# Order and size of the first transfers, and the place of early work, in a sliding-window attention kernel with a feed-forward stage

## The chip, the cores and the metric

The kernel runs on one core of a Trainium2 chip. The core has TensorE (PE: matmuls and transposes into PSUM; its weight loads are listed as PEld), VectorE (DVE), ScalarE (ACT), GpSimd (POOL) and SyncE (SP), each with its own instruction stream, and 16 DMA engines that move data between HBM and SBUF. Streams wait for each other by semaphores. The metric is the device time of one execution in microseconds.

## The reference

Attention over 8 batches of 8 heads, 576 positions, head size 64, where a position sees the positions at most 32 away, followed by a feed-forward layer on the 4608 tokens (512 features, 2048 hidden):

```
scores = q @ k^T / sqrt(64);  masked to |i - j| <= 32
attn   = softmax(scores);     y = attn @ v
x = y with the heads side by side          # 4608 x 512
h = x @ w_in                               # 4608 x 2048
g = h where h >= 1;  0 where h <= -1;  (h + 1)^2 / 4 between
out = g @ w_out                            # 4608 x 512
```

Inputs are float32; the kernel's transfers turn them into bfloat16 on the way in.

## The kernel before, in words

Everything is recorded in a fixed order (a manual schedule): each engine runs its instructions in the order in which the Python code gives them.

**Visits.** The main loop `for a in range(NF * NB + NF)` runs 152 visits. NB = 18 blocks of TB = 256 tokens, NF = 8 groups of 256 hidden columns. Visit a belongs to block t and group f (a = 8t + f). It makes `hp`, 256 hidden values of 256 tokens: 8 matmuls of 128x256 from `xT` (the attention's result, transposed) and 256 columns of `w_in` (line 441). ACT makes `rr` from hp (445), DVE makes `mx` (447) and then `gT` (448), the activated hidden values. So visits 0 and 1 read w_in's columns 0 to 511, visits 2 and 3 those from 512, visits 4 and 5 those from 1024, visits 6 and 7 those from 1536, and visit 8 starts the second block.

**Quarters.** `quarter(x)` (line 412) makes a quarter of the sum over hidden values of 128 output rows: 4 matmuls of 128x512 from gT and one of four pieces of `w_out`; x = 4 * (row group) + piece. After the fourth piece ACT copies the rows (417) and SP stores them. From visit 16 on each visit does the quarter a - 8; for the first two blocks the table `quarters` tells which visit does which. Quarters 3 and 7 are the first that read the fourth piece of w_out.

**Attention.** The long transfers of q and k (`load_long`, line 85) bring the first three batches in halves, four transfers each for q and for k and each half. `tpose` (179, 181) transposes them on TensorE into PSUM in two parts, 5 and 4 groups of columns, with one copy each into `qT` or `kT` (182). `scores` (218) and `scores8` (243) multiply q and k and take the exponential on ACT (226, 249, 251); the mask is either added beforehand by matmuls with `bias` (198, where `eng` is None) or multiplied afterwards by DVE (193, where `eng` is V). `sums` (284) multiplies with v and with ones; its `end` has ACT make the reciprocal in two steps (290, 291) and leaves to `muls` a DVE product that writes `xT` (296, 299); `flush` records the pending products. The table `ev`, filled by `at`, says in which visit each of these steps stands, and `tps` in which visit the transposes stand. Block 0 needs the first 256 positions of batch 0, which are done ahead of the loop; visit 8 needs the rest of batch 0 up to position 512, so the second halves of q and k of batch 0 are transposed in visit 1 and scored in visits 2 and 3, with sums in visits 3 to 5. Visit 16 needs the first sums of batch 1, which stand in visit 15. Two PSUM pools of two banks each, `ps_s` and `ps_n`, serve scores, sums and transposes in turn; `ps_o` holds quarters, and the tiles of visits 6 and 7; `ps_h` the other hp.

**Transfers.** All but the first q go through POOL's queue, in the order of lines 101 to 152: the first half of k and v of batch 0, then the list `w` (w_in in pieces, each half of the partitions apart, line 105) with the second half of q and k of batch 0 mixed in, then w_out (109) and the halves of batches 1 and 2. Later batches are loaded from within the loop (93, 101) and transposed by DMA (186).

**Warming.** `keep_warm` (318) issues matmuls whose results nobody reads.

Of the kernel before, what the change touches and what calls it, by code (L numbers as in the profile page):

```python
# [15 lines left out]
def kernel(  # L16
# [20 lines left out]
    B, H, S, D = q.shape  # L37
# [9 lines left out]

    const = ctx.enter_context(tc.tile_pool(name="const", bufs=1))
    nat = ctx.enter_context(tc.tile_pool(name="nat", bufs=2))
    qjp = ctx.enter_context(tc.tile_pool(name="qjp", bufs=2))  # L50
    ktp = ctx.enter_context(tc.tile_pool(name="ktp", bufs=3))
    ptp = ctx.enter_context(tc.tile_pool(name="ptp", bufs=2))
    smp = ctx.enter_context(tc.tile_pool(name="smp", bufs=2))
# [87 lines left out]
    def halves(b, half):  # L141
        return [(load_long, b, half, t, y) for t in range(2) for y in range(NY)]

    def put(todo):
        for fn, *x in todo:
            fn(*x)

    w = [(load_w_in, c, c + d, h) for c, d in ((0, 256), (256, 256), (512, 512), (1024, 512), (1536, 512)) for h in range(2)]
    x = halves(0, 1)
    put(w[:4] + x[:4] + w[4:5] + x[4:] + w[5:])  # L150
    mix(halves(1, 0), [(load_w_out, 0)])
    put([(load_w_out, 1), (load_w_out, 2)] + [(load_v, 1, n) for n in range(4)])
    mix(halves(1, 1), [(load_w_out, 3)])
# [102 lines left out]
    def sums(b, y1, lo, hi, pool=ps_n):  # L256

        bb = two_banks(pool)
        w = hi - lo
        todo = []  # L260
        if lo < MAIN:
            ys, D0 = (y1,), w
            for par in range(2):
                a0 = max(lo, 32 * par)
                off = 32 - 64 * par
                todo.append((None, a0 - lo, hi - lo, lambda a, h, par=par, a0=a0, off=off: (
                    pt[b][HD[a], h, y1, par, a0 + off:hi + off])))
                for c2 in range(4):
                    q0, q1 = max(0, 128 * c2 - off, lo), min(128 * c2 + 128 - off, hi)
                    if q0 < q1:  # L270
                        todo.append((NC * y1 + 2 * c2 + par, q0 - lo, q1 - lo, lambda a, h, par=par, q0=q0, q1=q1, off=off: (
                            pt[b][HD[a], h, y1, par, q0 + off:q1 + off])))
        else:
            ys, D0 = (0, 1), 2 * w
            todo.append((None, 0, 2 * w, lambda a, h: pt8[b][HD[a], h].rearrange("p y j -> p (y j)")))
            for y in ys:
                todo.append((NC * y + 8, y * w, y * w + w, lambda a, h, y=y: pt8[b][HD[a], h, y]))
                for c in (None, NC * y + 7):
                    todo.append((c, y * w, y * w + 64, lambda a, h, y=y: pt[b][HD[a], h, y, 1, 448:512]))
        for n, (c, c0, c1, p) in enumerate(todo):  # L280
            o = D0 if c is None else 0
            for a in range(2):
                for h in range(2):
                    nc.tensor.matmul(bb[HD[h], a, o + c0:o + c1], ones[HD[a]] if c is None else vn[b][HD[a], c, h],  # L284
                                     p(a, h), start=n == 0, stop=True, skip_group_check=True)

        def end():
            lr = smp.tile([128, 2, 256], FP, name="lr", bufs=1)
            rc = smp.tile([128, 2, 256], FP, name="rc")
            A.activation(lr[:, :, :D0], bb[:, :, D0:2 * D0], AF.Ln)  # L290
            A.activation(rc[:, :, :D0], lr[:, :, :D0], AF.Exp, scale=-1.0)  # L291
            r0 = (b * S + lo) % RING
            o = xT.rearrange("p (a y) t -> p a y t", a=2)[:, :, ys[0]:ys[-1] + 1, r0:r0 + w]
            if len(ys) == 1:
                o = o[:, :, 0]
                muls.append(lambda: V.tensor_mul(o, bb[:, :, :D0], rc[:, :, :D0]))  # L296
            else:
                like = "p a (y j) -> p a y j"
                muls.append(lambda: V.tensor_mul(o, bb[:, :, :D0].rearrange(like, y=2), rc[:, :, :D0].rearrange(like, y=2)))
        return end  # L300

    def flush():
        while muls:
            muls.pop(0)()
# [4 lines left out]
    def tp1(pool):  # L309
        if pool is ps_h:  # L310
            return pool.tile([128, 8, 128], BF, name="tp", tag="hp")
        return pool.tile([128, 2, 8, 128], BF, name="tp", tag="bb")[:, 0]

    def keep_warm(n, pool, tag):

        z = pool.tile([128, 512], FP, name="z", tag=tag)
        for _ in range(n):
            nc.tensor.matmul(z, warm[:, :128], warm, start=True, stop=True)
# [42 lines left out]

    NB = NT // TB
    NF = DFF // 256
    quarters = {11: ([], [0]), 12: ([], [1]), 13: ([], [2]), 14: ([], [4, 5]), 15: ([6], [3, 7])}
    ev, tps = {}, {}

    def at(a, *todo):

        ev.setdefault(a, []).extend(x for x in todo if x)

    def steps(b, cut):

# [2 lines left out]
                yield (sums, b, y1, lo, hi), (scores, b, (y1, y1 + 1), (0, 2), (2 * k, 2 * k + 2))  # L375
        yield (sums, b, 0, MAIN, S), (scores8, b)

    at(2, (scores, 0, (0, 1), (0, 2), (2, 4)), (scores8, 0, ps_o))
    at(3, (sums, 0, 0, TB, MAIN), (scores, 0, (1, 2), (0, 2), (2, 4)))
    at(4, (sums, 0, 1, TB, MAIN, ps_s))  # L380
    at(5, (sums, 0, 0, MAIN, S))
    seq = [x for b in range(1, B) for x in steps(b, 224)]
    at(15, seq[0][0], (*seq[1][0], ps_s))
    for n, a in enumerate((20, 22, 23, 27)):
        at(a, seq[2 + n][0])
    for n, a in enumerate((11, 12, 19, 20, 22, 26, 27)):
        at(a, seq[n][1])
    sl = [30, 32, 35, 39, 42, 45, 49, 52, 56, 59, 62, 65, 69, 73, 77, 81, 84, 88, 92]
    sl += [96, 99, 103, 106, 110, 113, 116, 120, 124, 128]
    for n, a in enumerate(sl):  # L390
        at(a, seq[6 + n][0], seq[7 + n][1] if n < len(sl) - 1 else None)
    for b, half, *a in ((0, 1, 1, 1.5), (1, 0, 9, 10), (1, 1, 17, 18), (2, 0, 24, 25), (2, 1, 28, 29)):
        for t in range(2):
            tps[a[t]] = [(b, 2 * half + part, t) for part in range(2)]
    loads, xps = {}, {}
    for b in range(LONG, B):
        a = sl[5 * (b - 1) - 7] - 17
# [7 lines left out]
    def quarter(x):  # L405

        tt, ff = divmod(x, 4)
        if tt not in op:
            op[tt] = ps_o.tile([128, DM], FP, name="op", tag="op"), []
        o, done = op[tt]  # L410
        for j in range(4 * ff, 4 * ff + 4):
            nc.tensor.matmul(o, gT[tt // 2][:, j, 128 * (tt % 2):128 * (tt % 2) + 128], w_out[:, j],  # L412
                             start=not done, stop=len(done) == 2 * NF - 1, skip_group_check=True)
            done.append(j)
        if len(done) == 2 * NF:
            osb = osp.tile([128, DM], FP, name="osb")
            A.copy(osb, o)  # L417
            nc.sync.dma_start(out=out[128 * tt:128 * tt + 128, :], in_=osb)

    for a in range(NF * NB + NF):  # L420
        t, f = divmod(a, NF)
        eng = None if a < 12 else V
        pre, post = quarters.get(a, ([], [a - NF] if a >= 2 * NF else []))
        for b, x in loads.get(a, []):
            if x < 2:
                load_nat(b, x)
            else:
                for n in range(4):
                    load_v(b, n)
        flush()  # L430
        if t < NB:
            if f == 0:
                gT[t] = gtp.tile([128, 2 * NF, TB], BF, name="gT", tag="gT")
            r0 = TB * t % RING
            if a in (6, 7):
                hp = ps_o.tile([128, 2, TB], FP, name="hp", tag="op")
            else:
                hp = ps_h.tile([128, 2, TB], FP, name="hp", tag="hp")
            for j in range(2):
                for n, kk in enumerate((0, 2, 1, 3)):  # L440
                    nc.tensor.matmul(hp[:, j], w_in[:, kk, 256 * f + 128 * j:256 * f + 128 * j + 128],  # L441
                                     xT[:, kk, r0:r0 + TB], start=n == 0, stop=n == 3)

            rr = ewp.tile([128, 2, TB], FP, name="rr")
            A.activation(rr, hp, AF.Relu, scale=0.5, bias=0.5)  # L445
            mx = ewp.tile([128, 2, TB], FP, name="mx")
            V.tensor_max(mx, hp, rr)  # L447
            V.scalar_tensor_tensor(gT[t][:, 2 * f:2 * f + 2], rr, 1.0, mx, op0=ALU.min, op1=ALU.mult)  # L448
        for x in pre:
            quarter(x)  # L450
        ends = []
        for fn, *x in ev.get(a, []):
            if fn is sums:
                ends.append(sums(*x))
            else:
                pool = (x.pop(),) if x[-1] in (ps_s, ps_n, ps_o) else ()
                fn(*x, eng, *pool)
        for end in ends:
            end()
        for x in post:  # L460
            quarter(x)
        for part in (a, a + 0.5):
            copies = [tpose(b, n, t, (A.copy, V.tensor_copy)[i if a > 15 else 0], tp1((ps_s, ps_n)[i]))
                      for i, (b, n, t) in enumerate(tps.get(part, []))]
            for x in copies:
                x()
        for x in xps.get(a, []):
            xpose(*x)

# [29 lines left out]
```

## Time and profile before

| what | us |
|---|---|
| median of 7 runs (322.29 to 324.14) | 323.01 |
| the profiled execution | 323.01 |
| its span, first to last instruction | 321.2 |
| PE busy in the span | 300.5 |
| DVE busy | 246.6 |
| ACT busy | 194.7 |
| L441 (visits' matmuls), busy | 150.2 |
| L412 (quarters), busy | 137.8 |
| mean granted TensorE clock | 0.992 |

Times in the profile count from the first instruction of the span. A row of the timeline reads: start, length, engine, line, operation, output <- input, shape, count, and in brackets how long the engine had stood idle and what ended it. "Time to landing" of a transfer counts from the start of its issue on the queue's engine to its last byte's signal. The clock is the share of full speed that TensorE was granted.

### The profile page before, as it was taken

The numbers are of one execution on the slowest core, as the hardware profiler recorded it, in microseconds if no ns is written. First come the engines' busy times: TensorE is split into PE (matmuls) and PEld (weight loads), VectorE is DVE, ScalarE is ACT, GpSimd is POOL, SyncE is SP. The second block draws the span as 40 slices with busy tenths as digits, with TensorE's granted clock in tenths as the row PEclk, the third lists the DMA queues.
The fourth block names the chain that finished last, engine by engine and source line by source line (L and its number), as shares of the span: only waits on it lengthen the run. The fifth ranks groups of instructions, "written<-read, shape, count | busy, mean of one in ns | idle before, by whom it ended". The sixth has DMA issues, their size and how long they took to land.

```text
span 321.2 us, 8493 instructions
## 1 busy us (share of the span) xinstructions
PE 300.5 (94%) x3599; PEld 202.4 (63%) x3643; DVE 246.6 (77%) x384; ACT 194.7 (61%) x320; POOL 86.2 (27%) x120
## 2 busy tenths in 40 slices
PE   8949899989999999999999999999999999999995
PEld 3536655566666666666666666666666666666652
DVE  2335975887888898888888888888888888887760
ACT  3648765676776566766666667566666766554421
POOL 8882826998303703221410300000000000000000
PEclk9998999999999999999999999999999999999999
DMA  9999898999999999929991945005320001000111
GB/s 147 139 157 181 126 170 130 193 165 164 151 157 156 169 156 175 165 51 103 190 158 48 109 90 125 35 33 108 81 63 33 35 35 36 33 35 33 47 53 65
DMA packets 121029, 34.52 MB, mean 107 GB/s; under 512 B 108704, under 2 KB 116128, under 8 KB 120992
## 3 DMA queue, kind: packets, MB, share of 16 engines
q0 software_dynamic: 92128, 18.06, 73.0%
q1 hardware_dynamic: 28864, 15.93, 21.5%
q8 instruction: 28, 0.46, 0.6%
q14 instruction: 9, 0.07, 0.1%
HBM read 36.70 MB, written 9.44 MB: 144 GB/s over the span
## 4 chain that ended last, share of the span: by engine, by line
PE 83%; DVE 4%; DMA 3%; ACT 3%; issue 3%; POOL 3%; POOLq 0%; ACTq 0%
PE hp L441 37%; PE op L412 36%; PE bb L284 6%; DMA w_in<-in_moe_w_in_dram 3%; PE bb L218 2%; DVE mx L447 1%; DVE gT L448 1%; PE tp L179 1%; POOL vn L101 1%; POOL kn L85 1%; ACT pt L226 1%; ACT lr L290 1%; ACT rc L291 1%; POOL w_in L105 1%; ACT rr L445 1%
## 5 line engine op out<-in xcount | busy, mean ns | idle before, releaser
L441 PE MATMUL hp<-xT,w_in 128*128 128x256 bf16 x1152 | 150.2, 274 | 2.9 <-DVE xT L296 0.9
L412 PE MATMUL op<-w_out,gT 128*128 128x512 bf16 x534 | 137.8, 379 | 5.8 <-issue 5.4
L445 ACT ACTIVATE rr<-hp 128x512 f32<-128x512 f32 x144 | 85.6, 595 | 91.0 <-PE hp L441 87.6
L441 PEld LDWEIGHTS <-w_in 128*128 128x128 bf16 x1152 | 112.1, 98 | 44.8 <-issue 3.5
L447 DVE TENSOR_TENSOR mx<-hp,rr 128x512 f32<-128x512 f32 x144 | 99.3, 690 | 42.2 <-ACT rr L445 40.0
L448 DVE SCALAR_TENSOR_TENSOR gT<-rr,mx 128x512 bf16<-128x512 f32 x144 | 99.6, 692 | 4.9
L412 PEld LDWEIGHTS <-gT 128*128 128x128 bf16 x576 | 53.3, 98 | 41.7
L226 ACT ACTIVATE pt<-bb 128x1024 bf16<-128x1024 f32 (+1 forms) x33 | 33.1, 1010 | 6.1 <-PE bb L218 4.9
L101 POOL DMA_DIRECT2D vn<-in_v_dram x32 | 27.6, 881 | 27.6 <-PE bb L218 26.5
L296 DVE TENSOR_TENSOR xT<-bb,rc 128x512 bf16<-128x512 f32 (+1 forms) x32 | 21.1, 658 | 11.3 <-ACT rc L291 10.8
L417 ACT COPY osb<-op 128x512 f32<-128x512 f32 x36 | 20.8, 581 | 11.6 <-PE op L412 11.2
L291 ACT ACTIVATE rc<-lr 128x512 f32<-128x512 f32 (+2 forms) x40 | 23.5, 587 | 1.3
L93 POOL DMA_DIRECT2D qn<-in_q_dram x10 | 12.3, 1244 | 41.7 <-DMA qT<-qn 41.7
L290 ACT ACTIVATE lr<-bb 128x512 f32<-128x512 f32 (+2 forms) x40 | 22.0, 550 | 1.5 <-PE bb L284 1.3
L193 DVE TENSOR_TENSOR pt<-pt,mask 128x1024 bf16<-128x1024 bf16 (+1 forms) x34 | 20.9, 616 | 0.2 <-ACT pt L226 0.2
L284 PE MATMUL bb<-pt,ones 64*64 64x256 bf16 (+3 forms) x352 | 19.5, 255 | 1.4 <-DVE xT L296 0.6
L284 PE MATMUL bb<-pt,vn 64*64 64x128 bf16 (+3 forms) x712 | 18.4, 204 | 0.6 <-issue 0.6
L284 PEld LDWEIGHTS <-vn 64*64 64x64 bf16 x712 | 16.8, 107 | 0.8 <-issue 0.8
L284 PEld LDWEIGHTS <-ones 64*64 64x64 bf16 x352 | 10.4, 105 | 10.3 <-issue 9.4
L85 POOL DMA_DIRECT2D kn<-in_k_dram x24 | 13.0, 551 | 12.7 <-DMA w_in<-in_moe_w_in_dram 5.3
L218 PE MATMUL bb<-qT,kT 64*64 64x128 bf16 x520 | 13.4, 220 | 0.8 <-DVE kT L182 0.8
L93 POOL DMA_DIRECT2D kn<-in_k_dram x10 | 12.1, 1223 | 3.3 <-DMA kT<-kn 2.5
(44 smaller groups left out, 97.4 us busy)
## 6 DMA issues: line engine op xcount, KB each, us to landing
out_dram<-osb SPq DMA_DIRECT2D x36, 256.0 KB, 2.3
vn<-in_v_dram POOLq DMA_DIRECT2D x32, 144.0 KB, 6.2
qn<-in_q_dram POOLq DMA_DIRECT2D x10, 288.0 KB, 7.2
kn<-in_k_dram POOLq DMA_DIRECT2D x10, 288.0 KB, 8.5
w_out<-in_moe_w_out_dram POOLq DMA_DIRECT2D x4, 512.0 KB, 10.3
kn<-in_k_dram POOLq DMA_DIRECT2D x24, 72.0 KB, 4.4
w_in<-in_moe_w_in_dram POOLq DMA_DIRECT2D x6, 256.0 KB, 7.2
qn<-in_q_dram POOLq DMA_DIRECT2D x20, 72.0 KB, 4.7
```

The costliest lines, as they stand in the source:

```text
L93: nc.gpsimd.dma_start(out=x[:, :, h], in_=src[b, NY * h:NY * h + NY].rearrange("y s d -> (y s) d") .rearrange("(u p) d -> p u d", p=128))
L101: nc.gpsimd.dma_start(out=vn[b][64 * a:64 * a + 64, :, h], in_=v[b, y:y + 2].rearrange("y s d -> (y s) d") .rearrange("(c r) d -> r c d", ...
L226: A.activation(p, ps[:, :, :128 * n].rearrange(like, y=m), AF.Exp, scale=D ** -0.5)
L284: nc.tensor.matmul(bb[HD[h], a, o + c0:o + c1], ones[HD[a]] if c is None else vn[b][HD[a], c, h], p(a, h), start=n == 0, stop=True, skip_g ...
L290: A.activation(lr[:, :, :D0], bb[:, :, D0:2 * D0], AF.Ln)
L291: A.activation(rc[:, :, :D0], lr[:, :, :D0], AF.Exp, scale=-1.0)
L296: muls.append(lambda: V.tensor_mul(o, bb[:, :, :D0], rc[:, :, :D0]))
L412: nc.tensor.matmul(o, gT[tt // 2][:, j, 128 * (tt % 2):128 * (tt % 2) + 128], w_out[:, j], start=not done, stop=len(done) == 2 * NF - 1, s ...
L441: nc.tensor.matmul(hp[:, j], w_in[:, kk, 256 * f + 128 * j:256 * f + 128 * j + 128], xT[:, kk, r0:r0 + TB], start=n == 0, stop=n == 3)
L445: A.activation(rr, hp, AF.Relu, scale=0.5, bias=0.5)
L447: V.tensor_max(mx, hp, rr)
L448: V.scalar_tensor_tensor(gT[t][:, 2 * f:2 * f + 2], rr, 1.0, mx, op0=ALU.min, op1=ALU.mult)
```

## The change

1. **Transfers.** The piece of w_in with columns 512 to 1023 is cut in two pieces of 256 columns (w_in's transfers go from 10 to 12). The second halves of q and k of batch 0 are issued together behind the four transfers of columns 0 to 511; before, q stood there, then one transfer of 512 columns, then k.
2. **Visit 1.** The second parts of q and k are copied out of PSUM by DVE instead of ACT, and four warming matmuls stand between q's transposes and k's.
3. **Visits 3 to 5.** The second scores of visit 3 go ahead of the sums there and use the pool ps_n; the three sums use ps_s, ps_n, ps_s. In visits 1 to 5 the pending products are recorded behind the visit's gT, and not at its start.
4. **Visits 9 to 15.** Quarters 0 and 4 move to visits 9 and 11 and quarters 1, 5, 2, 6 to 12, 13, 13, 14; 3 and 7 stay in 15. The scores of visits 11 and 12 go behind the visit's quarter, and both add their mask by matmuls (the border for `eng` moves from 12 to 14).
5. The transposes of later halves are entered in `ev` at half positions (9.5 and so on), which `run` serves behind the quarters as `tps` did. The unused pool `qjp` goes. From visit 16 on the order of instructions on PE, ACT and DVE is the same.

```diff
-    w = [(load_w_in, c, c + d, h) for c, d in ((0, 256), (256, 256), (512, 512), (1024, 512), (1536, 512)) for h in range(2)]
-    x = halves(0, 1)
-    put(w[:4] + x[:4] + w[4:5] + x[4:] + w[5:])
+    w = [(load_w_in, c, c + d, h) for c, d in ((0, 256), (256, 256), (512, 256), (768, 256), (1024, 512), (1536, 512))
+         for h in range(2)]
+    put(w[:4] + halves(0, 1) + w[4:])
...
-    quarters = {11: ([], [0]), 12: ([], [1]), 13: ([], [2]), 14: ([], [4, 5]), 15: ([6], [3, 7])}
+    quarters = [(9, 0), (11, 4), (12, 1), (13, 5), (13, 2), (14, 6), (15, 3), (15, 7)]
...
+    def through(b, half, t):
+        return [(tpose, b, 2 * half + part, t, part) for part in range(2)]
...
+    at(1, *through(0, 1, 0), (keep_warm, 4, ps_o, "op"))
+    at(1.5, *through(0, 1, 1))
     at(2, (scores, 0, (0, 1), (0, 2), (2, 4)), (scores8, 0, ps_o))
-    at(3, (sums, 0, 0, TB, MAIN), (scores, 0, (1, 2), (0, 2), (2, 4)))
-    at(4, (sums, 0, 1, TB, MAIN, ps_s))
-    at(5, (sums, 0, 0, MAIN, S))
+    at(3, (scores, 0, (1, 2), (0, 2), (2, 4), ps_n), (sums, 0, 0, TB, MAIN, ps_s))
+    at(4, (sums, 0, 1, TB, MAIN))
+    at(5, (sums, 0, 0, MAIN, S, ps_s))
...
-    for n, a in enumerate((11, 12, 19, 20, 22, 26, 27)):
+    for n, a in enumerate((11.5, 12.5, 19, 20, 22, 26, 27)):
         at(a, seq[n][1])
...
+    def run(pos):
+        todo = []
+        for fn, *x in ev.get(pos, []):
+            if fn is sums:
+                todo.append(sums(*x))
+            elif fn is tpose:
+                part = x.pop()
+                todo.append(tpose(*x, (A.copy, V.tensor_copy)[part if pos < 2 or pos > 16 else 0], tp1((ps_s, ps_n)[part])))
+                if part:
+                    while todo:
+                        todo.pop(0)()
+            elif fn is keep_warm:
+                keep_warm(*x)
+            else:
+                pool = (x.pop(),) if x[-1] in (ps_s, ps_n, ps_o) else ()
+                fn(*x, eng, *pool)
+        for end in todo:
+            end()
...
-        eng = None if a < 12 else V
+        eng = None if a < 14 else V
...
-        flush()
+        if a == 0 or a > 5:
+            flush()
...
+        flush()
+        run(a)
         for x in post:
             quarter(x)
-        for part in (a, a + 0.5):
-            copies = [tpose(b, n, t, (A.copy, V.tensor_copy)[i if a > 15 else 0], tp1((ps_s, ps_n)[i]))
-                      for i, (b, n, t) in enumerate(tps.get(part, []))]
-            for x in copies:
-                x()
+        run(a + 0.5)
```

More of the change, by code (lines that the diff above doesn't have):

```diff
@@ L49 @@
     nat = ctx.enter_context(tc.tile_pool(name="nat", bufs=2))
-    qjp = ctx.enter_context(tc.tile_pool(name="qjp", bufs=2))
     ktp = ctx.enter_context(tc.tile_pool(name="ktp", bufs=3))
@@ L363 @@
     NF = DFF // 256
-    quarters = {11: ([], [0]), 12: ([], [1]), 13: ([], [2]), 14: ([], [4, 5]), 15: ([6], [3, 7])}
-    ev, tps = {}, {}
+    quarters = [(9, 0), (11, 4), (12, 1), (13, 5), (13, 2), (14, 6), (15, 3), (15, 7)]
+    ev = {}
     def at(a, *todo):
         ev.setdefault(a, []).extend(x for x in todo if x)
+    def through(b, half, t):
+        return [(tpose, b, 2 * half + part, t, part) for part in range(2)]
     def steps(b, cut):
@@ L391 @@
         at(a, seq[6 + n][0], seq[7 + n][1] if n < len(sl) - 1 else None)
-    for b, half, *a in ((0, 1, 1, 1.5), (1, 0, 9, 10), (1, 1, 17, 18), (2, 0, 24, 25), (2, 1, 28, 29)):
+    for b, half, *a in ((1, 0, 9.5, 10.5), (1, 1, 17.5, 18.5), (2, 0, 24.5, 25.5), (2, 1, 28.5, 29.5)):
         for t in range(2):
-            tps[a[t]] = [(b, 2 * half + part, t) for part in range(2)]
+            at(a[t], *through(b, half, t))
     loads, xps = {}, {}
@@ L418, in quarter @@
             nc.sync.dma_start(out=out[128 * tt:128 * tt + 128, :], in_=osb)
+    def run(pos):
[16 more added lines that the diff above has]
+            end()
     for a in range(NF * NB + NF):
         t, f = divmod(a, NF)
-        eng = None if a < 12 else V
-        pre, post = quarters.get(a, ([], [a - NF] if a >= 2 * NF else []))
+        eng = None if a < 14 else V
+        post = [x for n, x in quarters if n == a] if a < 2 * NF else [a - NF]
         for b, x in loads.get(a, []):
@@ L429 @@
                     load_v(b, n)
-        flush()
+        if a == 0 or a > 5:
+            flush()
         if t < NB:
-            if f == 0:
+            if t not in gT:
                 gT[t] = gtp.tile([128, 2 * NF, TB], BF, name="gT", tag="gT")
@@ L448 @@
             V.scalar_tensor_tensor(gT[t][:, 2 * f:2 * f + 2], rr, 1.0, mx, op0=ALU.min, op1=ALU.mult)
[L449 to L459, printed above, removed]
+        flush()
+        run(a)
         for x in post:
             quarter(x)
-        for part in (a, a + 0.5):
-            copies = [tpose(b, n, t, (A.copy, V.tensor_copy)[i if a > 15 else 0], tp1((ps_s, ps_n)[i]))
-                      for i, (b, n, t) in enumerate(tps.get(part, []))]
-            for x in copies:
-                x()
+        run(a + 0.5)
         for x in xps.get(a, []):
```

## The prediction

> **What bounds the kernel now.** The profiled execution took 323.01 us, which is also the median of the runs shown; 321.2 us of it is the span between first and last instruction, and 1.8 us lie around it. I sum against 323.01. I first read the page's slices and the chain of work that ended last.
>
> ```profile
> PE   8949899989999999999999999999999999999995
> PEclk9998999999999999999999999999999999999999
> PE 83%; DVE 4%; DMA 3%; ACT 3%; issue 3%; POOL 3%; POOLq 0%; ACTq 0%
> ```
>
> A slice is 8 us. TensorE is full from the fifth slice on; the only hole is the third, 16 to 24 us, and behind it is the only dip of its clock. The chain is 83% PE and 3% DMA, and all that DMA is w_in. So only the first part can yield time. Next, the timeline of TensorE there, and the busy time by stretch (columns: PE, PEld, DVE, ACT, POOL, then granted clock, DMA share, GB/s):
>
> ```profile
> 17.47 0.69 PE L179 MATMUL tp<-ident,qn 128*64 128x128 bf16 x18 [0.32 <-DMA qn<-in_q_dram]
> 21.50 0.69 PE L179 MATMUL tp<-ident,kn 128*64 128x128 bf16 x18 [3.34 <-DMA kn<-in_k_dram]
> 22.85 1.87 PE L441 MATMUL hp<-xT,w_in 128*128 128x256 bf16 x8 [0.66 <-DMA w_in<-in_moe_w_in_dram]
> ...
> 34.57 1.91 PE L441 MATMUL hp<-xT,w_in 128*128 128x256 bf16 x16 [0.62 <-DVE xT L299]
> ```
> ```profile
> 15.98:19.39 3.41, 1.86 (x29) 1.36 (x27) 2.38 (x4) 2.55 (x4) 2.92 (x5) 1.00 1.09 145
> 19.39:22.81 3.42, 0.69 (x18) 0.56 (x18) 0.30 (x1) 0.80 (x2) 2.65 (x5) 1.00 1.15 169
> 22.81:26.22 3.41, 3.37 (x42) 2.20 (x43) 0.80 (x2) 1.60 (x3) 1.49 (x3) 0.50 1.09 141
> ```
>
> TensorE waits 3.34 us for k's second half, then 0.66 us for w_in's columns from 512. The stretch with 0.69 us of work in 3.42 is followed by one at clock 0.50, where visit 2 takes 1.87 us instead of 1.05 (the later visits). That looks like 4 to 5 us to be had. The question is whether they reach the end, so I followed TensorE to where the early part ends:
>
> ```profile
> 51.28 1.90 PE L412 MATMUL op<-w_out,gT 128*128 128x512 bf16 x7
> 53.02 0.38 PE L441 MATMUL hp<-xT,w_in 128*128 128x256 bf16 x2
> 54.09 0.81 PE L441 MATMUL hp<-xT,w_in 128*128 128x256 bf16 x6 [0.68 <-DVE xT L296]
> ```
>
> 51.28 starts quarters 3 and 7, the first that read the fourth piece of w_out. The DMA issues of 38.9 to 39.6 us, where that piece is issued (38.93, timeline of POOL), give its time to landing:
>
> ```profile
> w_out<-in_moe_w_out_dram POOLq DMA_DIRECT2D x1, 512.0 KB, 12.2
> vn<-in_v_dram POOLq DMA_DIRECT2D x1, 144.0 KB, 10.4
> ```
>
> 38.93 + 12.2 = 51.1 us: it lands 0.1 to 0.2 us before its first use. **TensorE has next to no room ahead of it there; whatever is won earlier ends in a wait for that piece, unless it lands earlier too.** The v beside it, issued at 38.10, lands at 48.5; visit 15's sums (50.43) read it.
>
> **What sets the landings.** POOL issues in order, and its waits show that an issue waits for the landing of the one eight before: the k at 33.54 waits for a w_out that was issued eight earlier (21.36 + 11.9 = 33.3). In the windows the DMA share is over 1.0 from 10 to 33 us and again from 36 to 51 us, with 0.61 between 33.05 and 36.46: a stream that is limited by its transfers, in the order of issue, with one hole set by that landing. After the first w_out everything to the fourth is the same order in both kernels, so the fourth moves as the first does: by d, the change in the time of the bytes ahead of it. These are the same bytes.
>
> **The change, part by part.**
>
> *Transfers.* q and k of the second half are issued behind the four small w_in pieces, so one 512-column piece (256 KB) no longer stands ahead of k. q's last lands at 12.98 + 4.4 = 17.3 as before. The k issues fall at about 14.0, 14.6, 15.1 and 16.2 (same waits: the four w_in pieces); the last of them lands 2.6 us after issue when nothing is ahead (the k at 33.54) and not before four times 0.36 us (72 KB at the 204 GB/s of 27 to 30 us) behind q, so at 18.8 instead of 16.68 + 4.7 = 21.4. w_in's 512 to 767 follow at about 20.7 (256 KB at 140 GB/s behind k) instead of 17.20 + 5.5 = 22.7, 768 to 1023 at 22.6, and from there as before: 1024 to 1535 whole at 26.4, the last at 20.77 + 10.1 = 30.8.
>
> *d.* Price of smaller pieces: from 12.9 to 13.5 us, small pieces alone, the stream makes 135 GB/s; with large ones 146 (20.7 to 21.3) to 170 (22 to 24). For 512 KB that is 3.9 us against 3.6 to 3.1: +0.3 to +0.8, +0.6 taken. Against it, the large piece issued at 14.00 lands at 19.9 (5.9 later), 2.5 us behind q's last, while large pieces land 2.0 apart (22.7 to 30.8 for four): some 0.5 us was lost there and should not be. d = 0.6 - 0.5 = **+0.1**. Ends: -0.5 (no price, loss gone) and +1.2 (the first four small pieces came in 5.2 us, from v's last landing at 6.77 + 3.9 = 10.7 to 15.9, so 1.3 each, against 2.0 for a large one: 2 x (2.6 - 2.0)).
>
> The Trainium skill speaks against this part: "DMA: Bandwidth & Descriptors", Bandwidth, advises batching to 1 MiB, and its section on the anatomy of one DMA gives each a fixed 2.0 us. Two more DMAs would by that, as an estimate, put d at 4.0 and the kernel near 326. But the k issued at 16.16 and 16.68 land half a microsecond apart here, the fixed part being hidden by the seven others in flight; I go by the rows.
>
> *Visit 1.* The second q and k copies go to DVE (0.71 us a COPY), behind gT of visit 1 (ends 19.69), so q's ends at 20.4 and the second k transposes, which need its PSUM, run at 20.4 to 20.7; k's copy ends at 21.5. ACT drops 0.60 each. Four warming matmuls add 4 x 0.22 = 0.9 us of PE in a wait (18.2 to 19.0). Cover: w_in's columns, due at 20.7; without it they would cost 0.2. Work in 19.39 to 22.81 is then about 2.0 us of 3.42 (transposes 0.7, visit 2 1.0, first scores 0.3); 1.86 kept the clock (row above), so I take 1.00, and visit 2 runs at 20.8 to 21.8.
>
> *Visits 3 to 8.* Visit 3 waits for w_in to 22.7, visit 4 to 26.4, visit 6 to 30.8 (before: 32.03). The re-pooled sums and the moved DVE multiplies (flush behind gT in visits 1 to 5) add no instruction; they only let the tail's multiply end at about 32.5 instead of 34.52. So of the lead that k's early landing gives, the wait for w_in's last piece takes part, and 2.0 us are left at visit 8: 32.6 instead of 34.57. DVE, packed from 30.8 to 42.7 before, starts that much earlier too.
>
> *Visits 9 to 15.* Two quarters move ahead, none is added; the scores of visit 12 take bias matmuls instead of a DVE mask: PE +0.2 us (4 of 0.05), DVE -0.68. TensorE took 34.57 to 50.43 = 15.9 us for this before; plus 0.2, it would be at the sums at 48.7 or earlier, and not before v at 48.5. The first scores and quarters read landed data: w_out's first at 33.3, second at 34.07 + 5.9 = 40.0 (quarter 1 at about 41), third at 43.6 (quarter 2 at about 44). If the 2.0 us were less by up to 1.2, nothing changes: the next term hides it.
>
> *The wait.* Sums end at 49.5, and the ACT and DVE chain behind them (3.0 us: 51.04 to 54.04 before) ends at 52.5. Quarters 3 and 7 wait for w_out to 51.15 + d, start 0.1 later at 51.25 + d, take 1.74 (51.28 to 53.02), and visit 16 takes 0.87 (a visit in the chain of the steady part): 53.86 + d. Before, it took from 53.02 to 54.90, its 0.68 us wait for xT included. That wait is what goes; the wait for w_out is late next. From visit 16 on, both orders are the same and TensorE leads; the next k lands at 52.52 + 2.4 = 54.9 and is read at about 59 (59.90 before).
>
> **Sum:** 54.90 - 53.86 - d = 1.04 - 0.1 = 0.94 us. 323.01 - 0.94 = **322.1 us**, -0.3%.
>
> **The rivals.**
> - *The stream gets ahead too* (d = -0.5 or lower, with less lost between pieces and TensorE 2 us ahead): at most what visit 8 gained, 323.01 - 2.0 = 321.0; at the bound d = -0.5, 321.5. For: dead time around 16 us. Against: the share is already over 1.0. Chance 0.14.
> - *Smaller pieces slow the stream* (slower): d = +1.2, the fourth w_out at 52.3. 323.01 - 1.04 + 1.2 = 323.2. It decides from d = 1.04. For: 1.3 us a small piece. Against: that stretch also follows v's small packets. 0.17, of which 0.05 beyond d = 2.
> - *The clock falls in the new wait.* TensorE stands 1.6 us before quarter 3; if the stretch 50.11 to 53.53 is too empty, 3.41 us at 0.50 follow: +1.7, 323.8; twice is 325.5. It decides somewhere between 0.69 us of work in a stretch, which lost the clock, and 1.86, which kept it. Against: that stretch would still hold about 1.8 to 2.2 us. 0.10.
> - *It does not do what it says*: k lands no earlier, because the eight-deep issue holds it. 323.01 + 0.2 = 323.2. The waits above speak against it. 0.04.
> - My forecast: 0.55, itself 321.5 to 322.9.
>
> **Numbers.** A measurement of this kernel tells about 0.3%, 1.0 us, from no change. Faster by that is below 322.04: nearly half of the forecast (0.28) and the first rival, 0.42. Slower is above 323.98: the clock case where it lasts or meets a d over 0.2 (0.07) and the far end of the small pieces (0.05), 0.12. The rest is 0.46. Range: 321.2, between the first rival's two times, to 323.8, the clock lost once; outside remain most of the doubled gain (0.07) and the 0.12 of slower.
>
> **What would show it.** Right: k's transposes at about 19 to 21 us; no stretch at clock 0.50 behind them; visit 8 at 32 to 33; a wait for w_out of 1 to 2 us before quarter 3; no xT wait in visit 16. Wrong: the fourth w_out's landing away from 51 us by over 0.6, or quarter 3 not waiting for it.

## The result, and the profile after

The changed kernel takes 322.02 us (median of 25 runs, 320.43 to 323.35); the kernel before, beside it, 323.55 (62 runs, 321.77 to 325.85). The ratio is 0.9953, 95% interval 0.994 to 0.9965. The profiled execution took 321.99 us, its span is 320.2; that is 1.0 us under the profiled execution of before, while the medians lie 1.5 us apart. The difference between these two numbers turned out to be half of the lesson.

The slices of the page: TensorE's hole in the third slice is smaller, and the dip of its clock behind it is gone.

```profile
PE   8974999989999999999999999999999999999995
PEclk9999999999999999999999999999999999999999
```

The timeline of TensorE in the changed kernel:

```profile
19.64 0.47 PE L178 MATMUL tp<-ident,kn 128*64 128x128 bf16 x10 [0.85 <-DMA kn<-in_k_dram]
20.41 0.41 PE L178 MATMUL tp<-ident,kn 128*64 128x128 bf16 x8 [0.30 <-DVE qT L181]
20.97 1.03 PE L466 MATMUL hp<-xT,w_in 128*128 128x256 bf16 x8
...
28.24 1.03 PE L466 MATMUL hp<-xT,w_in 128*128 128x256 bf16 x8 [3.02 <-DMA w_in<-in_moe_w_in_dram]
...
31.95 0.28 PE L283 MATMUL bb<-pt,ones 64*64 64x192 bf16 x4 [1.16 <-DVE xT L295]
...
32.37 3.81 PE L466 MATMUL hp<-xT,w_in 128*128 128x256 bf16 x32
36.01 1.03 PE L417 MATMUL op<-w_out,gT 128*128 128x512 bf16 x3
...
37.60 1.05 PE L466 MATMUL hp<-xT,w_in 128*128 128x256 bf16 x8
...
49.38 0.29 PE L283 MATMUL bb<-pt,ones 64*64 64x224 bf16 x4
...
50.92 1.89 PE L417 MATMUL op<-w_out,gT 128*128 128x512 bf16 x7 [0.62 <-DMA w_out<-in_moe_w_out_dram]
52.65 1.24 PE L466 MATMUL hp<-xT,w_in 128*128 128x256 bf16 x8
```

The rows of the kernel before with which visits 4, 6 and 10 and the sums of visit 15 are compared:

```profile
28.03 1.05 PE L441 MATMUL hp<-xT,w_in 128*128 128x256 bf16 x8
...
32.03 1.92 PE L441 MATMUL hp<-xT,w_in 128*128 128x256 bf16 x16
...
37.83 1.03 PE L441 MATMUL hp<-xT,w_in 128*128 128x256 bf16 x8 [0.72 <-DVE mx L447]
...
50.43 0.29 PE L284 MATMUL bb<-pt,ones 64*64 64x224 bf16 x4
```

k's wait fell from 3.34 to 0.85 us, and visit 2 starts 1.9 us earlier at full clock. But visit 4 (28.24) stands 3.02 us for w_in's columns from 1024 and starts 0.2 us later than before; visits 6 to 9 start at 32.37, where visit 6 started at 32.03 before. The early lead is gone there. It comes back at visit 10: before, TensorE stood 0.72 us ahead of it for DVE; now quarter 0 (36.01) runs ahead of it, visit 10 still starts 0.2 us earlier, and the sums of visit 15 start at 49.38 instead of 50.43. At the end of the early part quarter 3 waits 0.62 us for w_out, and visit 16 is done at 53.9 instead of 54.9. The fourth w_out, by the DMA issues of 38.8 to 39.5 us, lands at 38.82 + 12.1 = 50.9, 0.3 earlier than before:

```profile
w_out<-in_moe_w_out_dram POOLq DMA_DIRECT2D x1, 512.0 KB, 12.1
```

The wait of 1.16 us in visit 5 is explained by DVE's timeline: the product that frees the PSUM tile (xT, 31.28) stands behind mx and gT of visit 4, which had to wait for w_in, though its input was ready at 26.9 (ACT's rc).

```profile
29.94 0.69 DVE L472 TENSOR_TENSOR mx<-hp,rr 128x512 f32<-128x512 f32 x1 [3.56 <-ACT rr L470]
30.67 0.69 DVE L473 SCALAR_TENSOR_TENSOR gT<-rr,mx 128x512 bf16<-128x512 f32 x1
31.28 0.62 DVE L295 TENSOR_TENSOR xT<-bb,rc 128x448 bf16<-128x448 f32 x1
```

### The profile page after: what moved, and what is told of

Read it like the earlier page. It is cut to its first block, busy times and chain, and to the rows that moved or that the text cites. A ratio compares the mean times of both kernels' runs of the same rounds, so it can differ in the third digit from the quotient of the medians.

```text
span 320.2 us, 8507 instructions
## 1 busy us (share of the span) xinstructions
PE 300.2 (94%) x3606; PEld 201.7 (63%) x3651; DVE 247.3 (77%) x385; ACT 193.5 (60%) x318; POOL 87.4 (27%) x122
## 4 chain that ended last, share of the span: by engine, by line
PE 82%; DMA 4%; POOL 4%; DVE 4%; ACT 3%; issue 3%; POOLq 0%; ACTq 0%
PE hp L466 37%; PE op L417 36%; PE bb L283 5%; DMA w_in<-in_moe_w_in_dram 4%; PE bb L217 2%; PE tp L178 1%; POOL w_in L104 1%; POOL kn L84 1%; DVE gT L473 1%; DVE mx L472 1%; POOL vn L100 1%; ACT rr L470 1%; ACT lr L289 1%; DVE xT L295 1%; ACT rc L290 1%
## 5 line engine op out<-in xcount | busy, mean ns | idle before, releaser
L100 POOL DMA_DIRECT2D vn<-in_v_dram x32 | 27.5, 881 | 27.6 <-PE bb L217 26.4
L422 ACT COPY osb<-op 128x512 f32<-128x512 f32 x36 | 20.9, 581 | 11.6 <-PE op L417 11.2
L92 POOL DMA_DIRECT2D qn<-in_q_dram x10 | 12.3, 1244 | 40.1 <-DMA qT<-qn 40.1
L283 PE MATMUL bb<-pt,ones 64*64 64x256 bf16 (+3 forms) x352 | 19.5, 255 | 2.4 <-DVE xT L295 1.8
L84 POOL DMA_DIRECT2D kn<-in_k_dram x24 | 13.0, 551 | 9.6 <-DMA w_out<-in_moe_w_out_dram 3.8
L84 POOL DMA_DIRECT2D qn<-in_q_dram x20 | 11.0, 562 | 8.8 <-DMA w_in<-in_moe_w_in_dram 3.8
```

Of the source, the lines that this page charges most:

```text
L84: (eng or nc.gpsimd).dma_start(out=dst[b, half][32 * y:32 * y + 32], in_=src[b].rearrange("(h y) s d -> y h (s d)", h=2)[y] .rearrange("h ...
L100: nc.gpsimd.dma_start(out=vn[b][64 * a:64 * a + 64, :, h], in_=v[b, y:y + 2].rearrange("y s d -> (y s) d") .rearrange("(c r) d -> r c d", ...
```

## The experiments

Ratios are to the kernel before on the same chip. Theory A is the one on record: the transfers make the lead, the fourth w_out caps it. Theory B, formed on the trace after: the lead comes from the quarter that was put into the wait ahead of visit 10.

| kernel | ratio | 95% interval |
|---|---|---|
| changed | 0.9953 | 0.994 to 0.9965 |
| transfers alone | 0.9959 | 0.9938 to 0.9979 |
| places alone | 0.9981 | 0.9958 to 1.0005 |
| one large piece from 512 | 0.9993 | 0.9974 to 1.0013 |
| third piece read twice | 0.9939 | 0.9915 to 0.9964 |
| old quarters | 0.9932 | 0.9905 to 0.9958 |
| second w_out early | 0.9949 | 0.9925 to 0.9973 |
| products first | 0.9925 | 0.9898 to 0.9952 |
| products first, w_out early | 0.9958 | 0.9941 to 0.9975 |
| warming in visit 3 | 0.994 | 0.9919 to 0.9961 |
| no warming in visit 1 | 0.994 | 0.9915 to 0.9964 |
| all of w_in in small pieces | 0.9917 | 0.9901 to 0.9934 |
| four of these together | 0.9972 | 0.9955 to 0.9989 |

**Transfers alone, places alone.** The kernel before with the new list `w`, and the changed kernel with the old one.

> The kernel before with the changed list of transfers alone. Theory A (the early k and w_in make the lead, and the fourth piece of w_out caps it): most of the gain, 0.9965 or less of the time before, about 322.4 against 323.5; visit 8 starts clearly ahead of 34.57, and quarter 3 waits for w_out. Theory B (the lead is the quarter that was moved into the wait ahead of visit 10; the early transfers are eaten by the wait for w_in in visit 4): 0.998 to 1.001, with visit 2 some 2 us earlier but visit 10 within 0.4 us of 37.83, and sums of visit 15 within 0.4 us of 50.43.

> The changed kernel with the old list of transfers. Theory A: little is left of the gain, 0.998 to 1.001. Theory B: most of it stays, 0.9955 to 0.997, with the sums of visit 15 about 0.9 us ahead of 50.43 and quarter 3 right at the landing of the fourth w_out. Both expect the 3 us wait for k again, and a stretch at half clock only if the four warming matmuls do not hold it.

Theory A's number came: the transfers alone bring 0.9959, as good as the whole change, the places alone 0.9981, which can't be told from nothing. Theory B falls as the account of the gain. In the profiled run of the first, however, quarter 3 did not wait for w_out, which had landed at 50.4; so that cap was not what decided there.

```profile
50.97 1.90 PE L412 MATMUL op<-w_out,gT 128*128 128x512 bf16 x7
```

**One large piece.**

```diff
-    (512, 256), (768, 256), (1024, 512)
+    (512, 512), (1024, 512)
```

> The changed kernel with the columns 512 to 1023 in one transfer for each half of the partitions, behind q and k. If smaller pieces cost the stream (my price of +0.6 us), the fourth w_out lands about 0.6 us earlier and the time is 0.2 to 0.6 us under the changed kernel. If they cost nothing, its landing stays within 0.3 us; visit 2 then waits about 1 us longer for its columns, hidden by the wait for w_in in visit 4: 0.995 to 0.996.

The whole gain is gone: 0.9993. The fourth w_out landed at 50.6, against 50.9 in the changed kernel. One trace can't price small pieces so finely: in the seven kept traces of kernels with the changed kernel's list of transfers, on several chips, this landing lies anywhere from 49.3 to 52.4. A price does not show. What small pieces do is let visit 2 start: it needs 256 columns, and here waits until all 512 have landed (timeline), in a stretch of 3.42 us with 0.70 us of work, which half clock follows from 24.26 us on (busy time by stretch: PE, PEld, DVE, ACT, POOL, clock, DMA share, GB/s):

```profile
23.95 1.61 PE L466 MATMUL hp<-xT,w_in 128*128 128x256 bf16 x8 [2.71 <-DMA w_in<-in_moe_w_in_dram]
```
```profile
20.84:24.26 3.42, 0.70 (x18) 0.55 (x13) 0.72 (x1) 0.76 (x1) 1.33 (x4) 1.00 1.19 189
```

Visit 2 starts 3.0 us later than in the changed kernel, and visit 6 at 33.88; my "wait hidden by visit 4" was wrong.

**The cap at quarter 3.** In the first kernel quarters 3 and 7 read the third piece of w_out, `w_out[:, j - 4 if x in (3, 7) else j]`, so its first 256 output rows leave out the fourth piece's part. In the second the second w_out is issued earlier:

```diff
-    mix(halves(1, 0), [(load_w_out, 0)])
-    put([(load_w_out, 1), (load_w_out, 2)] + ...
+    mix(halves(1, 0), [(load_w_out, 0), (load_w_out, 1)])
+    put([(load_w_out, 2)] + ...
```

> Quarters 3 and 7 read the third piece of w_out in place of the fourth, so the first 256 output rows leave out that piece's part. If the wait for the fourth piece is what caps the gain (both theories), the 0.62 us wait before quarter 3 goes; but the chain from the sums of visit 15 to xT is next and lies only 0.4 us behind, so 0.2 to 0.6 us less than the changed kernel: 0.994 of the time before or a little less. If the cap is elsewhere, the time of the changed kernel, 0.9953.

> The changed kernel with the second piece of w_out issued among the first halves of batch 1, ahead of its last six. That should close the hole in the stream at 33 to 36 us (share 0.65) and bring v of batch 1 and the fourth w_out some 2 us forward (50.9 to about 49). If the fourth w_out caps the gain, quarter 3 no longer waits and the time falls by the 0.4 us that lie before the next limit, more where the landing is later than in the profiled run: 0.993 to 0.995 of before. If the early visits (2 to 8) set the end instead, the time of the changed kernel, 0.9953, with no wait for w_out and none gained. The k of batch 1 could land later than visit 10 needs it (36.1 now, read at 38.6).

Without the wait 0.9939, with the landing moved to 48.9, 0.9949: 0.5 and 0.1 us less than the changed kernel, where the intervals are 0.8 us wide to either side. So a gain does not show. In the profiled runs TensorE itself arrives at 50.2 or later (51.70 in the second, whose visit 4 waited 2.80 us and ran at half clock): the cap and the early visits lie almost on one another.

**Old quarters.** The list `[(11, 0), (12, 1), (13, 2), (14, 4), (14, 5), (15, 6), (15, 3), (15, 7)]` in the changed kernel.

> The changed kernel with the quarters of visits 9 to 15 back: 0 in 11, 1 in 12, 2 in 13, 4 and 5 in 14, 6 with 3 and 7 in 15 (behind the sums). If the quarter put into visit 9 fills the wait ahead of visit 10 (0.72 us for DVE before), visit 10 waits again and the end comes 0.5 to 0.9 us later: 0.997 to 0.9985. If that wait is only moved, because the fourth w_out caps the end anyway, the time stays: 0.995 to 0.996, quarter 6 filling the wait before quarter 3.

0.9932: moving the quarters ahead brings nothing that shows. Visit 10 waits 0.72 us for DVE again, but quarter 6, which in the kernel before stood ahead of the sums of visit 15, stands behind them here and covers the wait for xT; visit 16 runs without one. So here too a quarter fills a wait, only another one. (The profiled run is the slowest of its eight, 323.35 us against 320.84 to 322.33; its transfers land late throughout.)

```profile
38.32 1.03 PE L466 MATMUL hp<-xT,w_in 128*128 128x256 bf16 x8 [0.72 <-DVE mx L472]
...
51.81 2.54 PE L417 MATMUL op<-w_out,gT 128*128 128x512 bf16 x11 [0.16 <-issue]
54.19 1.05 PE L466 MATMUL hp<-xT,w_in 128*128 128x256 bf16 x8
```

**Products first.** The second flush's condition dropped, so that pending products come at a visit's start.

```diff
-        if a == 0 or a > 5:
-            flush()
+        flush()
```

> The changed kernel with the pending products of visits 1 to 5 recorded at a visit's start again, as before; all else stays. In the changed kernel the product of visit 3's sums stands behind gT of visit 4, which waits for w_in to 28.24, and the sums of visit 5 wait 1.16 us for it. With it ahead, the product should run at about 27, visit 5's wait go, visit 6 start at about 31 instead of 32.37. If the fourth w_out caps the end, little comes of it: 0.994 to 0.9953. If visits 2 to 8 set it, 0.9 to 1.2 us: 0.992.

In the trace the effect is as expected: the product runs at once, and visit 5 does not wait for it (DVE's timeline).

```profile
27.18 0.62 DVE L295 TENSOR_TENSOR xT<-bb,rc 128x448 bf16<-128x448 f32 x1 [0.54 <-ACT rc L290]
29.78 0.69 DVE L471 TENSOR_TENSOR mx<-hp,rr 128x512 f32<-128x512 f32 x1 [1.98 <-ACT rr L469]
```

The time, 0.9925, overlaps with the changed kernel's; and in this profiled run the clock fell just there, so visit 6 still began at 32.05. Together with the early w_out:

> The changed kernel with the products recorded at a visit's start and the second w_out moved forward. The first alone gave 0.9925 with quarter 3 at 50.33, right at the landing of the fourth w_out (50.29), the second alone landed it at 48.9 and gained nothing. If the two are limits in series, together they give 0.2 to 0.5 us more than the first alone: 0.991. If not, 0.9925.

0.9958, so the sum did not come. The moved w_out goes ahead of the last six transfers of q and k of batch 1, and TensorE waits for q:

```profile
36.19 0.69 PE L178 MATMUL tp<-ident,qn 128*64 128x128 bf16 x18 [0.83 <-DMA qn<-in_q_dram]
```

The second w_out came earlier at the price of transfers that are needed sooner.

**Warming.** Eight matmuls more in visit 3 (`at(3.5, (keep_warm, 8, ps_o, "op"))`), and none in visit 1.

> The changed kernel with eight more warming matmuls (1.7 us) behind visit 3, inside the 3 us wait for w_in ahead of visit 4. About half of the changed kernel's runs show a mean clock of 0.992 to 0.995, the others 1.0. If the clock falls in that wait and the half-clock stretch behind it costs time, most runs show 1.0 now and the median falls by 0.3 to 0.7 us: 0.993 to 0.9945. If it falls elsewhere (visits 1 to 3) or costs nothing because the fourth w_out caps the end, the share of such runs or the time stays.

> The changed kernel without the four warming matmuls of visit 1. Runs so far sort by mean clock: one whole stretch at half clock makes 0.995, two 0.989, and each costs about 1 us; before, 35 of 50 runs stood at 0.990 or less (median 324.4), the changed kernel has none there, 12 of 26 above 0.998 (321.5). If the gain is mainly the clock and the four matmuls hold it, most runs show 0.989 to 0.995 here and the time rises by 0.5 to 1.0 us: 0.997 to 0.999. If the earlier k alone holds it, the split of runs and the time stay: 0.995.

6 of 10 runs with the added matmuls stood at a clock above 0.998, against 12 of 26 of the changed kernel; without any, 2 of 12, and three lower than 0.9905, which the changed kernel never shows. So warming matmuls may hold the clock somewhat, on few runs. In the time neither differs from the changed kernel: not settled. In the profiled run with the added matmuls the clock fell after the stretch from 18.84 to 22.26 us (1.31 us of work), with the waits ahead of visit 2, where they do not reach.

**All of w_in in small pieces.**

```diff
-    (1024, 512), (1536, 512))
+    (1024, 256), (1280, 256), (1536, 256), (1792, 256))
```

> The changed kernel with the columns from 1024 on in pieces of 256 too (four more transfers). Visit 4 waits 3.0 us for columns 1024 to 1279 in the changed kernel; they should land at about 25 to 26 instead of 28.1, the wait fall to about 1 us and visit 6 start at 31 instead of 32.37. Theory: early visits set the end (w_out moved forward brought nothing), so 0.5 to 1 us is gained and fewer runs lose the clock: 0.991 to 0.994. Rival: smaller pieces cost the stream, the fourth w_out lands 0.6 to 1.2 us later and caps it: 0.9955 to 0.998.

0.9917, better than both kernels; its six runs lie between 320.55 and 321.31 us. TensorE's timeline:

```profile
25.65 1.03 PE L466 MATMUL hp<-xT,w_in 128*128 128x256 bf16 x8 [0.30 <-DMA w_in<-in_moe_w_in_dram]
...
29.73 0.28 PE L283 MATMUL bb<-pt,ones 64*64 64x192 bf16 x4 [1.54 <-DVE xT L295]
...
30.15 3.81 PE L466 MATMUL hp<-xT,w_in 128*128 128x256 bf16 x32
...
49.69 1.89 PE L417 MATMUL op<-w_out,gT 128*128 128x512 bf16 x7 [1.61 <-DMA w_out<-in_moe_w_out_dram]
51.41 1.04 PE L466 MATMUL hp<-xT,w_in 128*128 128x256 bf16 x8
```

Visit 4's wait is 0.30 us, visit 6 starts 2.2 us earlier, and now the recorded picture stands complete: 1.61 us of wait for w_out, then visit 16 with none. The stream did not become slower: w_in's last piece landed at 29.1 (30.6 in the changed kernel, 30.0 to 31.5 in the seven traces with its list), the fourth w_out at 38.05 + 11.6 = 49.7. The kernel without warming, which has the changed list and ran on the same chip, landed it at 49.3, so the stream did not become faster either. The rival expectation falls, by the time.

**Four together**: products first, early w_out, all pieces small, and the quarters of "old quarters".

> All of it: products at a visit's start, the second w_out forward, all of w_in in pieces of 256 columns, and the quarters of visits 9 to 15 as before (which gave 0.9932 alone). Visit 6 at 30 to 31, quarter 3 no later than 50, no xT wait in visit 16, since quarter 6 stands behind the sums: 0.988 to 0.991, about 1.5 us under the changed kernel. If smaller pieces slow the stream as much as they free the visits, 0.992.

0.9972, where 0.988 to 0.992 was expected. TensorE reached batch 1's q early and stood for it; half clock followed the emptied stretch (timeline, then busy time by stretch):

```profile
36.72 0.69 PE L178 MATMUL tp<-ident,qn 128*64 128x128 bf16 x18 [2.56 <-DMA kn<-in_k_dram]
```
```profile
34.60:38.02 3.42, 1.30 (x25) 1.18 (x26) 2.83 (x5) 1.04 (x3) 1.75 (x4) 1.00 1.19 193
38.02:41.43 3.41, 3.41 (x30) 2.33 (x29) 1.39 (x2) 2.52 (x4) 3.41 (x6) 0.50 1.89 175
```

The bracket names kn as what ended the wait, but the row's transposes read q, whose last transfer landed at 36.6. All 12 runs show a clock of 0.992 to 0.994.

## Why the prediction was right, step by step

That the time agrees so well (322.02 against 322.1) is in part luck: the forecast takes 0.94 us off 323.01, the median of seven runs; measured, 1.53 came off, from 323.55. Between the two profiled executions the end of the chain comes out nearly as summed (1.02 against 0.94), but steps on the way failed and made up for each other. Of the signs named, k's transposes came at 19.6 to 20.8 and no half clock behind them; visit 8 at 32 to 33, a wait of 1 to 2 us for w_out and a visit 16 without a wait did not.

- *Transfers.* k at 18.8: 19.5. Columns 512 at 20.7: 20.8; 768 at 22.6: 23.1; the last at 30.8: 30.6. But 1024 to 1535 "at 26.4": 28.1. That step failed by 1.7 us; in the seven traces with this list these columns land at 27.0 to 28.9. Why they come late, though the last columns come on time, is open.
- *d = +0.1.* Between the profiled runs, 50.88 - 51.15 = -0.3. But one list of transfers scatters by more than the whole range given for d: 49.3 to 52.4 with the changed list, and 49.6, not 51.15, in the kernel with the places alone, which has the old one. So neither d nor its term "+0.6 for smaller pieces" can be read from a pair of traces; on one chip, all pieces small and the changed list land it at 49.7 and 49.3. (The two k from which the fixed part was judged land at 21.03 and 21.37, a third of a microsecond apart and not half of one.) The Trainium skill ("DMA: Bandwidth & Descriptors", the anatomy of one DMA) gives each DMA a fixed part of about 2.0 us; six more transfers, if it were paid for each in turn, would by that, as an estimate, cost 12 us. That does not show here: the first w_out landed at 32.4 with all pieces small and, on the same chip, at 32.3 with the changed list.
- *Visits 3 to 8.* "They only let the tail's multiply end at about 32.5": it ended at 34.2, and visit 8 started at 34.3 instead of the 32.6 of the forecast. I counted instructions of the moved flush and not what it was put behind: a product that was ready waits for a visit that waits for a transfer, and it holds a PSUM tile that visit 5 needs (1.16 us).
- *Visits 9 to 15.* From visit 8 to the sums the sum allows 16.1 us (15.9 + 0.2); it took 15.1 (34.3 to 49.4). The quarter put ahead of visit 10 fills the 0.72 us that TensorE stood there before, which the sum does not count. That made up for most of the lead lost at visit 8.
- *The wait for w_out.* 0.62 us, not 1.6, because TensorE came at 50.3, not 49.5. With d = -0.3 the sum has visit 16 end at 53.56; it ended at 53.89. 0.2 us of that is a wait for xT (the row of visit 16 is 1.24 us long, 1.04 without a wait); the rest is in the sum itself: its 0.87 for a visit is the distance from one start to the next, while the 54.90 that it is taken from is the end of a row. Gain between the profiled executions 1.02, forecast 0.94.
- *The clock.* I took the profiled execution of before as the kernel. Here are all runs with a granted clock on record, sorted by its mean over the run (one whole stretch of 3.41 us at half clock makes 0.995, two make 0.989):

| mean clock | before: runs, median us | changed: runs, median us |
|---|---|---|
| over 0.9985 | none | 12, 321.47 |
| 0.9935 to 0.9985 | 9, 322.69 | 10, 322.50 |
| 0.9905 to 0.9935 | 17, 323.21 | 4, 322.10 |
| under 0.9905 | 55, 324.14 | none |

The second and third row both stand for one whole stretch: in the three kept traces with 0.992 the rest is a piece at the end of the span, behind the last matmul, where it costs nothing (before: from 319.77 us, the last matmul ends at 317.3). So two thirds of the runs of before have two stretches or more, and none is without; the profiled one (0.992) was among the better. The change takes away about one stretch a run, and a stretch goes with about 1.0 us in either kernel. Among runs with one stretch 0.7 us is left between the kernels (before 26 runs, 323.08; changed 14, 322.37). The other kernels mostly sort alike: two stretches in 6 of 12 runs with one large piece (0.9993), 7 of 12 with the places alone (0.9981), 4 of 12 with the transfers alone (0.9959), none of 6 with all of w_in in small pieces (0.9917); but 3 of 12 without warming (0.994). That the clock makes the larger part of the gain is argued from this sorting and from visit 2 (1.87 us at half clock, 1.03 at full); the waits that empty a stretch cost time themselves, and the runs that meant to move the clock alone did not settle it.

- *Rivals.* "The clock falls in the new wait" looked at the wrong wait. In six kept traces with the changed kernel's pieces of w_in half clock occurs, and it always starts earlier: in three after the wait ahead of visit 4 (transfers alone, second w_out early, products first), in three after the waits of visits 1 and 2 (third piece, warming in visit 3, no warming). With all pieces small, where the wait ahead of visit 4 is 0.30 us, the lowest of six runs is at 0.994 and the other five at 0.998 or more.

## What to carry to other kernels

Cut a load into the pieces in which it is first used and issue them in the order of use: here 256 columns a visit. Each wait of about 3 us that this removed was worth 1.2 to 1.3 us of the time; no re-placing of work showed a gain clear of noise over the kernel that it was put into. A landing read from one trace is no price: look at it in several, since here it scattered by 3 us over runs and chips with one list of transfers. A transfer moved forward takes its time from those that it passes, so look up when each of these is needed before it is moved. Where a product frees a buffer, what stands ahead of it on its engine counts, not its own length. Sort repeated runs by the granted clock before one profiled run is taken for the kernel.

## What the runs showed of the hardware

The clock is granted for stretches of 3.41 us whose place differs from run to run, and the clock of a stretch goes with the work in the one before. Cut at each run's own changes, stretches at full clock with 0.61, 0.69, 0.70, 1.30, 1.31, 1.45, 1.53 and 1.57 us of TensorE work were followed by half clock, and those with 1.57, 1.65, 1.71 and more kept it. The two at 1.57, first the changed kernel, whose next stretch is at full clock, then the one with products first:

```profile
23.65:27.06 3.41, 1.57 (x54) 1.10 (x51) 1.82 (x3) 3.00 (x6) 0.26 (x1) 1.00 1.18 184
27.06:30.48 3.42, 2.24 (x43) 1.85 (x44) 0.54 (x1) 1.14 (x2) 1.60 (x3) 1.00 1.24 205
```
```profile
26.23:29.65 3.42, 1.57 (x37) 1.25 (x38) 1.03 (x2) 1.38 (x3) 1.38 (x3) 1.00 1.24 204
29.65:33.06 3.41, 3.41 (x41) 2.27 (x42) 2.84 (x5) 2.61 (x6) 0.76 (x2) 0.50 1.20 200
```

So the border for keeping the clock lies at about 46% of a stretch, not at an empty one. To come back from half clock took more in the one case on record: in the profiled run of the places alone a stretch at half clock with 2.08 us of busy time was followed by a second one at half clock (the two rows of it overlap a little):

```profile
23.08:26.49 3.41, 2.08 (x12) 1.21 (x16) 0.60 (x1) 0.59 (x2) 1.27 (x3) 0.50 1.11 150
26.00:29.90 3.90, 3.90 (x54) 2.31 (x56) 1.39 (x2) 2.47 (x5) 1.49 (x3) 0.50 1.19 192
```

The Trainium skill ("TensorE: Matmul & The Clock Gate", Part 1) gives the free-running window of 3413 ns, which agrees; it has the clock fall after an idle window, and here windows with 1.3 to 1.57 us of matmuls lost it as well.
